# Attention with rotary embedding, then two feed-forward layers: k of two heads turned in one go, its second copy made by DMA

## The chip, the cores and the metric

The kernel runs on one core of a Trainium2 chip. The metric is the device time of one execution in microseconds; the time given is the median over several runs.

## The reference

The inputs q, k and v are float32 of shape (batch 4, heads 8, sequence 576, head dimension 64). Two feed-forward layers follow, with 2304 tokens, width 512 and inner width 2048.

```python
q_rot, k_rot = (rotate(q), rotate(k))        # rotary embedding over the 64 columns
scores = scale * np.matmul(q_rot, k_rot.transpose(0, 1, 3, 2))
scores = scores - np.max(scores, axis=-1, keepdims=True)
attn = np.exp(scores)
attn = attn / (np.sum(attn, axis=-1, keepdims=True) + 1e-09)
x = np.matmul(attn, v)                        # tokens (b, s) in rows, (h, d) in columns
h = x @ w_in;   x = (h - tanh(h)) @ w_out
h = x @ w_in2;  x = (h * sigmoid(h)) @ w_out2
```

## The kernel before

The attention works on 16 pairs of heads, one after the other, and each pair on nine steps. A step makes the scores of 128 queries of one head against all 576 keys. Steps 0 to 7 take the two heads in turn over the first 512 queries, and step 8 takes the last 64 queries of both heads. In step g TensorE makes the scores of g, turns the probabilities of step g - 2 (function `transposes`, LAG = 2), and then multiplies turned probabilities of the pair before with v (`pv`). VectorE takes the row maximum, ScalarE the exp (`exps`). The scores lie in two PSUM buffers, so the scores of step g need the exp of step g - 2 to be done. All other PSUM results of this part (turned probabilities, turned q and k, turned and spread reciprocals) share one ring of three buffers with the tag "tp".

The order of the work is written out by hand: each engine does its instructions in the order of the program text, and the one queue of SyncE (SP) that issues nearly all DMAs does so too. A wait of one instruction holds up all that stands behind it on that engine or queue.

While a pair is in work, the next pair's q and k are prepared. GpSimd rotates them (`rope_ops`, five units: q of each head, k of each head, and the remaining 64 rows of the sequence of q and k of both heads); a list of these operations is worked off over the steps, and `rope_upto` forces it up to a unit. Then TensorE turns them at the end of the steps that `QK_AT` names, so that the head dimension lies in the partitions: step 1 does q of both heads, step 3 k of the first head, step 5 k of the second, step 6 the remaining rows.

The scores are made in a split form. Each number is kept as a high part of the float32r type and the remainder. For q the high part of one head stands in 64 partitions and its remainder in the other 64 of the tile `qs`. So k must stand in both halves of the partitions, and there are two tiles of it, `kh` with the high part and `kl` with the remainder; one product with each gives q times k. To have k in both halves, `rope_dup` copies the rotated k beside itself on GpSimd before it is turned, and one turn of 128 columns yields it twice. `qk_high` turns a unit on TensorE and evicts its high parts on ScalarE at once; `qk_low` makes the remainders on VectorE one step later, after that step's row maximum. Only then is the ring buffer free.

During the attention, VectorE, ScalarE and GpSimd also convert weights of the feed-forward part from 64-bit floats, mostly in steps 7, 8 and 0. The weights come in loads of 512 KB that SP issues.

Of the kernel before, what the change touches and what calls it, by code (L numbers as in the profile page):

```python
# [8 lines left out]
F32 = mybir.dt.float32  # L9
# [4 lines left out]
ACTF = mybir.ActivationFunctionType  # L14
# [15 lines left out]
def kernel(  # L30
# [13 lines left out]
    nc = tc.nc  # L44
    B, H, S, D = q.shape
# [5 lines left out]
    NJ = S // 128  # L51
    REM = S - 128 * NJ
    MAIN = 128 * NJ
# [14 lines left out]
    PE, ACT, DVE, POOL = nc.tensor, nc.scalar, nc.vector, nc.gpsimd  # L68
# [141 lines left out]
    TPB = 3  # L210
    NPV = 4 * (NJ + 1)
    Q0 = 256
    QK_AT = {1: 0, 3: 1, 5: 2, 6: 3}
    ON_DVE = ((1, 1),)
    R_AT = (2, 4, 7)
    PV_N = (4, 0, 4, 2, 0, 4, 0, 4, 2)
# [1 line left out]
    def attention(conv, on_rope_done, on_scores_near, on_scores_done):  # L218
# [51 lines left out]
        def rope_ops(i, n, eng):  # L270
            st = {}

            def begin():
                rot = rot_t.setdefault(i, {})
                xm, xr = raw_t[i]
                if n < 2:
                    if n == 0:
                        rot[0] = rp.tile([128, NJ, 2, D], F32, tag="aq", name="aq", bufs=1)
                    st["o"] = rot[0][:, :, n, :]
                elif n < 4:  # L280
                    rot[n - 1] = rp.tile([128, NJ, 2, D], F32, tag="ak", name="ak", bufs=2)
                    st["o"] = rot[n - 1][:, :, 0, :]
                else:
                    rot[3] = rp.tile([128, 2, 2, D], F32, tag="ar", name="ar", bufs=1)
                    st["o"] = rot[3][:, :, 0, :]
                if n < 4:
                    st["b"] = rp.tile([128, NJ, D], F32, tag="bm", name="bm", bufs=3)
                    st["x"] = xm[n // 2][:, n % 2].rearrange("p (j d) -> p j d", j=NJ)
                    t = csk if n // 2 else csq
                    st["c"], st["s"] = t[:, 0], t[:, 1]  # L290
                else:
                    st["b"] = rp.tile([128, 2, D], F32, tag="br", name="br", bufs=1)
                    st["x"] = xr
                    st["c"], st["s"] = (csr[:, e].unsqueeze(1).to_broadcast([128, 2, D]) for e in range(2))
                eng.tensor_tensor(out=st["o"], in0=st["x"], in1=st["c"], op=ALU.mult)

            def cross():
                def halves(t):
                    return t.rearrange("p j (e d) -> p j e d", e=2)

                eng.tensor_tensor(out=halves(st["b"]), in0=halves(st["x"])[:, :, ::-1, :], in1=halves(st["s"]),
                                  op=ALU.mult)

            def add():
                eng.tensor_tensor(out=st["o"], in0=st["o"], in1=st["b"], op=ALU.add)

            return [begin, cross, add]

        def rope_dup(i, u):
            if u > 0:  # L310
                a = rot_t[i][u]
                if i:
                    POOL.tensor_copy(out=a[:, :, 1, :], in_=a[:, :, 0, :])
                else:
                    ACT.activation(out=a[:, :, 1, :], in_=a[:, :, 0, :], func=ACTF.Copy)

        def qk_alloc(i):
            qk_t[i] = [qkp[i % 2].tile([128, 2 * S + (REM if nm != "qs" else 0)], F32R, tag=nm, name=nm, bufs=1)
# [4 lines left out]
        KM = (slice(0, MAIN), slice(2 * S - MAIN, 2 * S))  # L323
        KO = (0, 2 * S - MAIN)
        up, dn = slice(0, 64), slice(64, 128)

        def qk_high(i, u):
            src = rot_t[i][u]
            qs, kh, kl, qr = qk_t[i]
            tp = ps.tile([128, 512], F32, tag="tp", name="tpq", bufs=TPB)  # L330
            for j in range(NJ if u < 3 else 2):
                PE.transpose(tp[:, j * 128:(j + 1) * 128], src[:, j].rearrange("p e d -> p (e d)"), ident)  # L332
            if u == 0:
                parts = [(qs[up, 0:MAIN], tp[up], qs[dn, 0:MAIN]), (qs[dn, S:S + MAIN], tp[dn], qs[up, S:S + MAIN])]
            elif u < 3:
                parts = [(kh[:, KM[u - 1]], tp, kl[:, KM[u - 1]])]
            else:
                t4 = tp[:, 0:256].rearrange("p (h s) -> p h s", h=2)
                parts = [(qr[up, h, h * 64:h * 64 + 64], t4[up, h, 0:64], qr[dn, h, h * 64:h * 64 + 64])
                         for h in range(2)]  # L340
                kc = slice(MAIN, MAIN + 128)
                parts.append((kh[:, kc].rearrange("p (h s) -> p h s", h=2), t4[:, :, 64:128],
                              kl[:, kc].rearrange("p (h s) -> p h s", h=2)))
                parts.append((kh[:, 2 * S:], t4[:, 1, 64:128], kl[:, 2 * S:]))
            for hi, t, lo in parts:
                ACT.activation(out=hi, in_=t, func=ACTF.Copy)  # L346
            return parts
# [32 lines left out]
        def exps(g):  # L380
            i, n = divmod(g, NTI)
            if n == 0:
                sum_t[i] = ap.tile([128, NTI], F32, tag="sums", name="sums", bufs=2)
            sc, st = s_t.pop(g), st_t.pop(g)
            h = tiles[n][0]
            if h != 1:
                p_t[g] = ap.tile([128, 2, S], F32, tag="p", name="p", bufs=2)
            else:
                p_t[g] = p_t[g - 1]
            p = p_t[g][:, h % 2]  # L390
            ACT.activation(out=p.rearrange("p (e s) -> p e s", e=2), in_=sc[:, :, 0:HALF],  # L391
                           func=ACTF.Exp, bias=st, accum_out=sum_t[i][:, n:n + 1])
# [127 lines left out]
        def rope_upto(i, n):  # L520
            while rq and rq[0][:2] <= (i, n):
                rq.pop(0)[2]()
# [23 lines left out]
                f()  # L546
        qk_alloc(0)
        rope_dup(0, 1)
        first = qk_high(0, 1)
        rope_dup(0, 3)  # L550
        first += qk_high(0, 0)
        first += qk_high(0, 3)
        for n in (0, 1, 5):
            qk_low([first[n]])
        parts = []
# [6 lines left out]
        while True:  # L562
            i, n = divmod(g, NTI)
            more = i + 1 < NP
            if 0 < i < NP and n == 2:
                load_v(i)
            if i + 2 < NP and n == 5:
                rope_upto(i + 1, 4)
                load_qk(i + 2)
                rope_push(i + 2)  # L570
            d = g - LAG - NTI
            i2, n2 = divmod(d, NTI)

            live = g < G

            if live:
                scores(g)
                if more and n == 0:
                    qk_alloc(i + 1)
                if g == 0:  # L580
                    parts.extend(first[2:5] + first[6:] + qk_high(0, 2))
            if 0 <= g - LAG < G:
                rest(g - LAG, g)
            if live:
                row_max(g)
            qk_low(parts)
            parts.clear()
            if 0 <= g - LAG < G:
                transposes(g - LAG)

            if more and QK_AT.get(n) == 0:
                rope_upto(i + 1, 1)
            elif more and n + 1 in QK_AT:
                rope_upto(i + 1, QK_AT[n + 1] + 1)
                rope_dup(i + 1, QK_AT[n + 1])
            if live:
                for _ in range(2 if n % 3 else 1):
                    if rq:
                        rq.pop(0)[2]()

            if 0 < i <= NP:
                at = R_AT if i < NP else (1, 2, 2)
                if n == 0:
                    recips(i - 1)
                if n == at[0]:
                    recip_rows(i - 1)
                for e in (1, 0):
                    if n == at[2 - e]:
                        recip_spread(i - 1, e)
            if d >= 0:  # L610
                if n2 == 0:
                    pvq.extend((i2, m) for m in range(NPV))
                for _ in range(PV_N[n2] if live else NPV // 2):
                    if pvq:
                        pv(*pvq.pop(0))
            rate = (CONV_RATE[n] if i else RATE_0) / 2 if live else 0.0
            conv.run(rate)
            if more and n in QK_AT:
                parts.extend(qk_high(i + 1, QK_AT[n]))
            if live:  # L620
                exps(g)
            conv.run(rate)
            if g == G - NTI:
                es_rope.close()
                es_even.close()
                on_rope_done()
            if g == G - SPLIT_AT:
                on_scores_near()
            if g == G - 1:
                es_odd.close()  # L630
                es_sc.close()
                on_scores_done()
            if g >= G:
                on_tail(g - G)
            if d > 0 and i2 == NP - 1 and not pvq:
                break
            g += 1
# [262 lines left out]
```

## Time and profile before

| what | value |
|---|---|
| time, median of 3 runs | 1146.62 us (1146.53 to 1146.91) |
| the profiled execution: its time, its span | 1147.64 us, 1145.9 us |
| share of the span that an engine is busy | TensorE 98%, weight load 79%, VectorE 69%, ScalarE 58%, GpSimd 23% |
| granted TensorE clock | 0.999 over the span |
| DMA | 98.94 MB, most of it on SP's queue, whose packets take 26.3% of 16 engines' span |
| attention, first to last scores | 13.1 to about 328 us of the span |

The span is the time from the first to the last instruction of the one profiled execution. The share of busy time is an average over the attention and the feed-forward part, which have different limits; a change in the attention is read from rows of the attention.

### The profile page before, as it was taken

How to read it: one execution, taken by the hardware profiler on the slowest of the kernel's cores; microseconds unless marked ns; L12 is line 12 of the kernel's file. 1: busy time of each engine (PE TensorE's matmuls, PEld its weight loads, DVE VectorE, ACT ScalarE, POOL GpSimd, SP SyncE). 2: the span in 40 equal slices, each digit the busy share in tenths (PEclk: the TensorE clock that was granted, in tenths of full speed). 3: DMA queues.
4: the chain of work that ended last, by engine and by line, in shares of the span. 5: the costliest groups of instructions: out<-in, count | busy, mean ns of one | idle time of the engine just before them, and what ended most of it. 6: DMA issues, size and time to landing. Idle time of an engine off the chain costs nothing.

```text
span 1145.9 us, 16928 instructions
## 1 busy us (share of the span) xinstructions
PE 1119.5 (98%) x6032; PEld 902.6 (79%) x6032; DVE 785.3 (69%) x1385; ACT 659.2 (58%) x1431; POOL 268.4 (23%) x359
## 2 busy tenths in 40 slices
PE   5999999999999999999999999999999999999998
PEld 4777777777778889888888898888888888888887
DVE  7778788787858978888899979876544533323323
ACT  4888888788866757766666657534343323222221
POOL 6566676666300101111001001111000000000000
PEclk9999999999999999999999999999999999999999
DMA  4133323232311223221333332432232203122012
GB/s 130 47 99 84 113 68 110 89 94 86 100 64 42 92 74 111 96 89 56 111 129 110 111 120 84 147 111 92 75 110 74 74 1 111 37 74 93 31 44 74
DMA packets 69588, 98.94 MB, mean 86 GB/s; under 512 B 13952, under 2 KB 50432, under 8 KB 67712
## 3 DMA queue, kind: packets, MB, share of 16 engines
q1 hardware_dynamic: 69344, 97.61, 26.3%
q8 instruction: 47, 0.77, 0.3%
q14 instruction: 37, 0.30, 0.1%
q10 hardware_dynamic: 160, 0.26, 0.1%
HBM read 74.25 MB, written 23.59 MB: 85 GB/s over the span
## 4 chain that ended last, share of the span: by engine, by line
PE 91%; DVE 4%; ACT 3%; issue 1%; DMA 0%; SPq 0%; POOL 0%; DVEq 0%; ACTq 0%
PE acc L761 35%; PE hp L685 35%; PE x L498 7%; PE tpp L466 4%; PE sc L364 3%; PE sc L365 2%; PE tpq L332 2%; PE sc L371 1%; ACT p L391 1%; DVE st L377 1%; ACT kh L346 1%; PE sc L446 1%; PE tpb L418 0%; DMA xm<-in_q_dram 0%; DVE wa L136 0%
## 5 line engine op out<-in xcount | busy, mean ns | idle before, releaser
L685 PE MATMUL hp<-xh,win 128*128 128x512 f32 (+1 forms) x1280 | 391.7, 371 | 0.0
L696 ACT ACTIVATE t<-hp 128x512 f32<-128x512 f32 (+1 forms) x160 | 89.0, 557 | 409.7 <-PE hp L685 400.0
L730 DVE TENSOR_TENSOR gl<-t,gh 128x512 fp32r<-128x512 f32 (+1 forms) x160 | 105.9, 662 | 259.5 <-ACT gh L728 259.2
L685 PEld LDWEIGHTS hp<-xh,win 128*128 128x128 f32 x1280 | 233.7, 188 | 46.8 <-issue 1.3
L685 PE MATMUL hp<-xl,win 128*128 128x512 f32 (+1 forms) x640 | 237.0, 370 | 0.0
L761 PE MATMUL acc<-gh,wout 128*128 128x512 f32 (+1 forms) x640 | 196.7, 372 | 1.2 <-ACT u L700 1.2
L761 PE MATMUL acc<-wout,gh 128*128 128x512 f32 x576 | 181.0, 395 | 0.0
L377 DVE TENSOR_REDUCE st<-sc 128x1 f32<-128x576 f32 x144 | 108.7, 755 | 60.0 <-PE sc L446 34.9
L685 PEld LDWEIGHTS hp<-xl,win 128*128 128x128 f32 x640 | 120.2, 188 | 23.2
L761 PEld LDWEIGHTS acc<-gh,wout 128*128 128x128 f32 x640 | 116.7, 188 | 24.9 <-ACT u L700 1.6
L761 PEld LDWEIGHTS acc<-wout,gh 128*128 128x128 f32 x576 | 107.1, 188 | 24.4
L761 PE MATMUL acc<-gl,wout 128*128 128x512 f32 (+1 forms) x320 | 118.9, 372 | 0.0
L153 POOL TENSOR_TENSOR win<-wa,win 128x512 fp32r<-128x512 f32 x32 | 45.4, 1419 | 292.5 <-ACT win L149 292.5
L761 PE MATMUL acc<-wout,gl 128*128 128x512 f32 x288 | 113.8, 395 | 0.0
L391 ACT ACTIVATE p<-sc,st 128x576 f32<-128x576 f32 x144 | 107.0, 743 | 9.4 <-DVE pr L434 7.2
L153 POOL TENSOR_TENSOR wout<-wa,wout 128x512 fp32r<-128x512 f32 x32 | 43.8, 1367 | 284.2 <-ACT wout L149 272.5
L432 ACT ACTIVATE pt<-tpp 128x512 f32<-128x512 f32 x144 | 86.1, 598 | 28.2 <-PE tpp L466 27.4
L728 ACT ACTIVATE gh<-t 128x512 fp32r<-128x512 f32 (+1 forms) x160 | 93.7, 586 | 1.5 <-PE acc L761 1.5
L364 PE MATMUL sc<-kh,qs 128*128 128x288 f32 x256 | 85.4, 348 | 7.1 <-ACT p L391 5.1
L466 PE MATMUL tpp<-ident,p 128*128 128x128 f32 x576 | 87.1, 274 | 0.0
L498 PE MATMUL x<-pt,vm 128*64 128x256 f32 (+1 forms) x512 | 75.8, 418 | 2.1 <-DVE xs L507 1.9
L364 PEld LDWEIGHTS sc<-kh,qs 128*128 128x128 f32 x256 | 49.2, 192 | 34.2 <-ACT p L391 17.8
(112 smaller groups left out, 1798.5 us busy)
## 6 DMA issues: line engine op xcount, KB each, us to landing
raw<-in_moe_w_in_dram SPq DMA_DIRECT2D x32, 512.0 KB, 3.6
raw<-in_moe_w_out_dram SPq DMA_DIRECT2D x32, 512.0 KB, 3.6
xin<-xd SPq DMA_DIRECT2D x14, 1024.0 KB, 4.8
pd<-xo SPq DMA_DIRECT2D x34, 256.0 KB, 2.7
xo<-pd SPq DMA_DIRECT2D x34, 256.0 KB, 4.9
xm<-in_k_dram SPq DMA_DIRECT2D x16, 256.0 KB, 2.9
xm<-in_q_dram SPq DMA_DIRECT2D x16, 256.0 KB, 3.0
vm<-in_v_dram SPq DMA_DIRECT2D x16, 256.0 KB, 2.9
```

The source lines that it names most:

```text
L153: POOL.tensor_tensor(out=w[:, 1], in0=self.val.pop(j), in1=w[:, 0].bitcast(F32), op=ALU.subtract)
L364: PE.matmul(sc[:, e, 0:HALF], lhsT=l, rhs=kh[:, c], start=True, stop=False)
L377: DVE.tensor_reduce(out=st, in_=s_t[g][:, :, 0:HALF], op=ALU.max, axis=AX.XY, negate=True)
L391: ACT.activation(out=p.rearrange("p (e s) -> p e s", e=2), in_=sc[:, :, 0:HALF], func=ACTF.Exp, bias=st, accum_out=sum_t[i][:, n:n + 1])
L432: ACT.activation(out=dst, in_=src, func=ACTF.Copy)
L466: PE.transpose(tp[:, cc * 128:(cc + 1) * 128], p[:, p0 + cc * 128:p0 + (cc + 1) * 128], ident)
L498: PE.matmul(x[o, 0:w], lhsT=l, rhs=r, start=(cc == 0), stop=(cc == NJ))
L685: PE.matmul(hp, lhsT=w[:, a, ws], rhs=bb, start=(n == 0), stop=(n == 3 * KD - 1))
L696: ACT.activation(out=t, in_=hp, func=ACTF.Tanh, scale=0.5 if l else 1.0)
L728: ACT.activation(out=gh, in_=t, func=ACTF.Copy)
L730: DVE.tensor_tensor(out=gl, in0=t, in1=gh.bitcast(F32), op=ALU.subtract)
L761: PE.matmul(acc, lhsT=a, rhs=bb, start=(fi == 0 and n == 0), stop=(fi == NH - 1 and n == 2))
```

## The change

The rotated k of both heads of the next pair is laid side by side in one tile and turned once, so that the first head comes out in the upper 64 partitions and the second in the lower 64. The remaining rows of q and k are treated likewise: one turn instead of two. High parts and remainders are then made of each head in its own 64 partitions alone, and eight DMAs from SBUF to SBUF, issued on SP's queue in step 6, bring each head's `kh` and `kl` to the other 64 partitions, and the remaining rows of the second head to a second place. GpSimd's copies are gone. The turns stand in steps 1, 3 and 5, and step 6 has none; k of both heads must be rotated by step 3. In each step ScalarE does the exp first and the evictions of turned q and k after it. The first pair is prepared as before.

```diff
-    QK_AT = {1: 0, 3: 1, 5: 2, 6: 3}
+    QK_AT = {1: 0, 3: 1, 5: 2}
...
+                elif n < 4 and i:
+                    if n == 2:
+                        rot[1] = rp.tile([128, NJ, 2, D], F32, tag="ak", name="ak", bufs=2)
+                    st["o"] = rot[1][:, :, n - 2, :]
...
-                    st["o"] = rot[3][:, :, 0, :]
+                    st["o"] = rot[3][:, 0] if i else rot[3][:, :, 0, :]
...
-                if i:
-                    POOL.tensor_copy(out=a[:, :, 1, :], in_=a[:, :, 0, :])
-                else:
-                    ACT.activation(out=a[:, :, 1, :], in_=a[:, :, 0, :], func=ACTF.Copy)
+                ACT.activation(out=a[:, :, 1, :], in_=a[:, :, 0, :], func=ACTF.Copy)
...
+        def qk_turn(i, u):
+
+            src = rot_t[i][(0, 1, 3)[u]]
+            qs, kh, kl, qr = qk_t[i]
+            tp = ps.tile([128, 512], F32, tag="tp", name="tpq", bufs=TPB)
+            for j in range(NJ if u < 2 else 1):
+                PE.transpose(tp[:, j * 128:(j + 1) * 128], src[:, j].rearrange("p e d -> p (e d)"), ident)
+            if u == 0:
+                return [(qs[up, 0:MAIN], tp[up], qs[dn, 0:MAIN]), (qs[dn, S:S + MAIN], tp[dn], qs[up, S:S + MAIN])]
+            if u == 1:
+                return [(kh[up, KM[0]], tp[up], kl[up, KM[0]]), (kh[dn, KM[1]], tp[dn], kl[dn, KM[1]])]
+            k0, k1 = slice(MAIN, S), slice(S, S + REM)
+            return [(qr[up, 0, 0:64], tp[up, 0:64], qr[dn, 0, 0:64]),
+                    (qr[dn, 1, 64:128], tp[dn, 0:64], qr[up, 1, 64:128]),
+                    (kh[up, k0], tp[up, 64:128], kl[up, k0]), (kh[dn, k1], tp[dn, 64:128], kl[dn, k1])]
+
+        def k_copies(i):
+            for t in qk_t[i][1:3]:
+                nc.sync.dma_start(out=t[dn, 0:S].bitcast(F32), in_=t[up, 0:S].bitcast(F32))
+                nc.sync.dma_start(out=t[up, S:2 * S].bitcast(F32), in_=t[dn, S:2 * S].bitcast(F32))
+                for o in (up, dn):
+                    nc.sync.dma_start(out=t[o, 2 * S:].bitcast(F32), in_=t[dn, S:S + REM].bitcast(F32))
...
+            return parts
+
+        def qk_evac(parts):
             for hi, t, lo in parts:
                 ACT.activation(out=hi, in_=t, func=ACTF.Copy)
             return parts
...
             qk_low(parts)
             parts.clear()
+            if more and n - 1 == max(QK_AT):
+                k_copies(i + 1)
...
-                rope_upto(i + 1, QK_AT[n + 1] + 1)
-                rope_dup(i + 1, QK_AT[n + 1])
+                rope_upto(i + 1, QK_AT[n + 1] + 2)
...
             if more and n in QK_AT:
-                parts.extend(qk_high(i + 1, QK_AT[n]))
+                parts.extend(qk_turn(i + 1, QK_AT[n]))
             if live:
                 exps(g)
+            qk_evac(parts)
```

## Rows read from the trace of the kernel before

**Rows 1.** Busy time of each engine, pairs 1 to 14; then clock, DMA share, GB/s

```profile
33.59:307.89 274.30, 268.43 (x1991) 205.42 (x1991) 217.35 (x440) 227.99 (x577) 175.36 (x268) 1.00 0.29 86
```

**Rows 2.** Timeline of TensorE, twelfth pair (start us, us, what)

```profile
242.51 0.66 PE L332 MATMUL tpq<-ident,ak 128*128 128x128 f32 x4
242.92 0.38 PE L364 MATMUL sc<-kh,qs 128*128 128x288 f32 x1
...
244.57 0.40 PE L364 MATMUL sc<-kh,qs 128*128 128x288 f32 x1 [0.23 <-ACT p L391]
...
245.67 0.42 PE L418 MATMUL tpb<-rt,sel 128*128 128x128 f32 x2
...
248.56 0.38 PE L364 MATMUL sc<-kh,qs 128*128 128x288 f32 x1
248.78 0.29 PE L365 MATMUL sc<-kl,qs 128*128 128x288 f32 x1
```

**Rows 3.** Timeline of TensorE, last pair: first products of steps 6 and 7

```profile
320.68 0.40 PE L364 MATMUL sc<-kh,qs 128*128 128x288 f32 x1
...
321.67 0.38 PE L364 MATMUL sc<-kh,qs 128*128 128x288 f32 x1
```

**Rows 4.** Timeline of ScalarE, twelfth pair

```profile
241.93 0.60 ACT L432 ACTIVATE pt<-tpp 128x512 f32<-128x512 f32 x1 [0.93 <-PE tpp L466]
243.20 0.60 ACT L346 ACTIVATE kh<-tpq 128x512 fp32r<-128x512 f32 x1 [0.68 <-PE tpq L332]
243.69 0.74 ACT L391 ACTIVATE p<-sc,st 128x576 f32<-128x576 f32 x1
...
244.89 0.32 ACT L346 ACTIVATE qr<-tpq 64x64 fp32r<-64x64 f32 x2
...
245.36 0.74 ACT L391 ACTIVATE p<-sc,st 128x576 f32<-128x576 f32 x1
```

**Rows 5.** Timeline of VectorE, twelfth pair

```profile
241.49 0.76 DVE L377 TENSOR_REDUCE st<-sc 128x1 f32<-128x576 f32 x1 [1.39 <-PE sc L446]
...
243.72 0.76 DVE L377 TENSOR_REDUCE st<-sc 128x1 f32<-128x576 f32 x1 [0.53 <-PE sc L365]
244.40 0.68 DVE L351 TENSOR_TENSOR kl<-tpq,kh 128x512 fp32r<-128x512 f32 x1
...
246.29 0.35 DVE L351 TENSOR_TENSOR qr<-tpq,qr 64x64 fp32r<-64x64 f32 x2
```

**Rows 6.** Timelines of GpSimd and TensorE, step 3 of the fifth pair

```profile
97.39 0.74 POOL L305 TENSOR_TENSOR ak<-ak,bm 128x256 f32<-128x256 f32 x1
...
98.47 0.60 PE L332 MATMUL tpq<-ident,ak 128*128 128x128 f32 x4
```

**Rows 7.** Timeline of SP's queue, ninth and twelfth pairs (issue, not transfer)

```profile
175.96 1.12 SPq L267 DMA_DIRECT2D vr<-in_v_dram  x2
...
179.08 0.63 SPq L251 DMA_DIRECT2D xr<-in_q_dram  x1
...
243.62 0.42 SPq L512 DMA_DIRECT2D xd<-xs  x1
244.14 7.76 SPq L115 DMA_DIRECT2D raw<-in_moe_w_out_dram  x2
```

**Rows 8.** DMA issues: count, KB each, median us from issue to landing

```profile
xm<-in_q_dram SPq DMA_DIRECT2D x16, 256.0 KB, 3.0
...
xd<-xs SPq DMA_DIRECT2D x32, 128.0 KB, 2.0
...
xd<-xs SPq DMA_DIRECT2D x16, 32.0 KB, 1.7
```

**Rows 9.** Timeline of all engines, step 4 of the ninth pair

```profile
178.66 0.60 PE L466 MATMUL tpp<-ident,p 128*128 128x128 f32 x4
...
178.87 0.75 ACT L391 ACTIVATE p<-sc,st 128x576 f32<-128x576 f32 x1
```

**Rows 10.** Timeline of VectorE, thirteenth pair: a weight's first conversion

```profile
266.89 0.42 DVE L129 TENSOR_SCALAR wa<-raw 128x512 int32<-128x512 int32 x1
```

More of the change, by code (lines that the diff above doesn't have):

```diff
@@ L548, in attention @@
         rope_dup(0, 1)
-        first = qk_high(0, 1)
+        first = qk_evac(qk_high(0, 1))
         rope_dup(0, 3)
-        first += qk_high(0, 0)
-        first += qk_high(0, 3)
+        first += qk_evac(qk_high(0, 0))
+        first += qk_evac(qk_high(0, 3))
         for n in (0, 1, 5):
@@ L580, in attention @@
                 if g == 0:
-                    parts.extend(first[2:5] + first[6:] + qk_high(0, 2))
+                    parts.extend(first[2:5] + first[6:] + qk_evac(qk_high(0, 2)))
             if 0 <= g - LAG < G:
```

## The prediction

> **What bounds the kernel now.** I read the busy times of a stretch first, then the timelines of single engines over one pair of heads, then the queue that issues DMAs. Over pairs 1 to 14 of the attention TensorE is busy 268.4 of 274.3 us, ScalarE 228.0, VectorE 217.4, GpSimd 175.4 [rows 1]. [...] So a step of this stretch lasts as long as TensorE's list for it, unless something holds that list up.
>
> [...]
>
> In the twelfth pair, the quiet one that I work with, the four turned tiles of the next pair stand at the end of steps 1, 3, 5 and 6. Step 5 ends with four transposes for the second head's k, from 242.51 to 242.92. Step 6 ends with two for the rests; the scores of step 7 begin only at 244.57, after 0.23 us of waiting for an exp [rows 2]. In the last pair nothing is turned, and there step 6 takes 321.67 − 320.68 = 0.99 us [rows 3], against 244.57 − 242.92 = 1.65 [rows 2]. TensorE's own list and that wait make the step, then, and taking work from it shortens it.
>
> **The change part by part**, per pair; 15 pairs are turned this way.
>
> *Transposes.* 14 become 9. Step 5 has one instead of four. The four cost 242.92 − 242.51 = 0.41 us, so one some 0.11; saved 0.30 (bounds: 0, if one costs as much as the group, and 0.41). Step 6 has none: 1.65 − 0.99 = 0.66 saved, as the last pair shows. Together 0.96, times 15 = 14.4 us. Steps 1 and 3 keep their four.
>
> *Exp before the evictions.* The 0.66 holds only if the scores of step 7 find their buffer free, which the exp of step 5 frees. Before, ScalarE waited 0.68 us for the transposes, evicted k at 243.20 and began that exp at 243.69 [rows 4]. Now it can begin when the eviction of 241.93 has passed (0.49 us a piece, by 243.20 to 243.69) and the row maximum of 241.49 is there (242.25) [rows 4, 5]: at 242.42, done by 243.16. Step 7 now wants to begin at 242.92 − 0.30 + 0.99 = 243.61. So the wait goes. In steps 1 and 3 the exp also comes earlier, but nothing waited for it, and I give it nothing.
>
> *Evictions and remainders.* Eight evictions and eight remainders a pair, as before, only elsewhere. Step 3 evicts two halves of 64 rows where it had one tile, some 0.5 us more on ScalarE and 0.7 on VectorE in step 4; both idle just after, 0.93 us before 241.93 and 1.39 before 241.49 [rows 4, 5], and that hides it. Uncovered it would cost up to 0.7 a pair. The four small remainders of the rests move from step 7 to step 6. VectorE reaches them after step 6's row maximum, which began 243.72 − 242.92 = 0.80 after the scores: now at 242.62 + 0.80 + 0.68 = 244.10. Four at 0.35 for two last till 244.80 [rows 5]. They free the last of three tp buffers, and by the order of allocation the next in need of it is the spread of reciprocals of step 7, which TensorE reaches 245.67 − 244.57 = 1.10 after step 7's start, at 244.71. So a new wait of some 0.10 (bounds 0 and 0.4): −1.5 us in all.
>
> *GpSimd* loses three copies. The second head's rotated k must now be there by step 3, not step 5. In the tightest pair it ends at 97.39 + 0.74 = 98.13 and step 3's transposes begin at 98.47 [rows 6]; a copy that stood ahead of it goes, so the margin grows. Cost nothing; if the cover failed, a few tenths of a us in some pairs.
>
> *Eight DMAs a pair.* This is the part without a row of its own: SBUF to SBUF, 64 rows. For kh and then for kl: 64 x 576 words (144 KB) down, 144 KB up, and two small ones. They go into SP's queue in step 6, behind the stores of the attention's output. The last of those issued at 243.62, and the next DMA followed at 244.14 [rows 7]. By then the evictions that kh needs are done (four take 245.36 − 244.89 = 0.47 after the exp, so 243.63) [rows 4], and kl's remainders (244.80) come in time for the fifth. Issue costs per DMA: the nearest rows are 64-row loads, 1.12 for two, or 0.56, and 0.63; the 128-row store took 0.42 [rows 7]. I take 0.56, since rows of 64 partitions are nearest. kl's first copy, the fifth, goes out at 244.14 + 4 x 0.56 = 246.38.
>
> Landing: a 128 KB store takes 2.0 us, a 32 KB one 1.7, a 256 KB load 3.0 [rows 8]. I take 2.0, the nearest size: 248.38. Bounds 1.7 and 3.0.
>
> Who needs it: dependencies here go by region (a transposition of one half of a p tile ran at 178.66, before the exp that writes the other half, issued earlier, at 178.87 [rows 9]), so the next pair's first scores wait for kl's first copy alone. They begin at 243.61 + (248.56 − 244.57 = 3.99) + 0.10 = 247.70, and their first product with kl 0.22 later (248.78 − 248.56) [rows 2], at 247.92. TensorE then stands 248.38 − 247.92 = 0.46 us at each pair's start: −6.9 us. Behind it on TensorE stands everything, so this is lost in full.
>
> What waits behind the eight in SP's queue: the weight load that went at 244.14 goes some 4.5 us later. What it brings is first converted at 266.89 [rows 10], so nothing is lost. The feed-forward part after the attention is unchanged and runs on TensorE without a gap, so what the attention saves arrives at the end.
>
> *Sum.* Per pair 0.30 + 0.66 − 0.10 − 0.46 = 0.40, times 15 = 6.0 us. The profiled execution took 1147.64 (span 1145.9 and 1.7 around it), 1.0 above the median of 1146.62; 1141.6 for such an execution, and **1140.6** for the median.
>
> **The rivals.**
>
> *The copies land in time.* If they issue in the store's 0.42 [rows 7] and land in 2.0, kl's first is there at 244.14 + 1.68 + 2.0 = 247.82, before 247.92. Then 0.86 x 15 = 12.9: **1133.7**. For it: these copies never leave the core's memory. Against it: each 64-row row seen took over 0.5 to issue.
>
> *64 rows move at half the rate.* From 32 to 128 KB a store takes 0.3 us more [rows 8], so 1.6 fixed and 0.3 for each 96 KB at 128 rows. At half that rate 144 KB takes 0.9, and the copy lands after 2.5, at 248.88. The wait is 0.96, the pair loses 0.10, in all +1.5: **1148.1**, no change that can be measured. For it: no large 64-row transfer is in the trace that would exclude it. Against it: the same rows say that most of the 2 us is fixed.
>
> [...]
>
> *The copies are late for good (the other side).* Place: the same wait at the next pair's start. At 0.63 an issue and the 3.0 of the 256 KB load the copy lands at 244.14 + 2.52 + 3.0 = 249.66, the wait is 1.74, the pair loses 0.88: +13.2, **1159.8**. It decides from a landing past 248.78 on, where 0.86 is used up; past 248.93 the loss can be measured (2.3 us over 15 pairs). For it: three large copies, two of them just ahead, share the DMA engines with it. Against it: those engines are busy 29% in this stretch [rows 1].
>
> **How the numbers follow.** Wait of about half a us, 1140.6: 0.45. In time, 1133.7: 0.22. Half rate, 1148.1: 0.17. Late, up to 1159.8: 0.16. A measurement of this kernel tells about 0.2%, 2.3 us, from no change. The first two are faster (0.67), the third is the same (0.17), the fourth slower (0.16). The range runs from 1132, the second case with no wait for remainders (14.4 saved), to 1149, just past the third; the fourth is left out. The likeliest case's own range is 1136 to 1144.
>
> **What would show it.** Step 6 at 0.99 and step 5 some 0.30 shorter show the transposes right. The exp of step 5 ahead of the small evictions, and no wait for it before step 7, show the reordering right. At the start of each pair, TensorE idle before the first product with kl, released by a DMA, shows the copies' price: 0.46 expected, nothing in the second case, about 1 in the third, more in the fourth. A wait for VectorE before the spread of step 7 of 0.1 shows the buffer's. I am wrong if step 1 to 5 grow, if GpSimd's rope is late for step 3, or if the wait at the pair's start moves elsewhere, such as to later steps' kh.

## The result and the profile after

The changed kernel takes 1164.32 us (median of 4 runs, 1161.76 to 1165.68) against 1146.76 (1146.53 to 1147.12): a ratio of 1.0150, 95% interval 1.0134 to 1.0166. It is slower by 17.6 us where 6.0 us of gain were predicted. The profiled execution has a span of 1163.0 us, 17.1 more than before. From the first scores of the last step to the end of the span both traces need the same 821.7 us, so the whole difference arises in the attention.

The windows view over pairs 1 to 14 of the kernel after:

```profile
33.95:324.68 290.73, 270.11 (x1923) 200.94 (x1922) 230.88 (x440) 238.24 (x578) 163.29 (x225) 0.99 0.42 115
```

Against [rows 1] the stretch is 16.4 us longer with TensorE busy for about as long: 270.1 of 290.7 us, where it was 268.4 of 274.3. TensorE now stands still for 20.6 us instead of 5.9. The DMA engines are busy 42% instead of 29%. The mean granted clock is 0.99, not 1.00; outside two stretches, which are shown below, it is 1.00.

Where it stands still, the waits view of the kernel after says (engine and line that waits, on what; total us, times, longest), PEld and PE being the weight load and the product of one and the same matmul:

```profile
PEld sc L392 <- DMA kl<-kl: 21.2, 15, 2.7
PE sc L392 <- DMA kl<-kl: 18.0, 15, 2.5
```

The kernel before has no such wait. It comes 15 times, once for each pair that is turned in the new way, and TensorE loses 18.0 us in it.

Twice more was lost than the length of the wait. The first products with kl in the second and third pair, with the wait before them, and then the windows view of the stretches in which the clock was granted at 0.50, soon after each of these two products:

```profile
36.82 0.40 PE L392 MATMUL sc<-kl,qs 128*128 128x288 f32 x1 [2.49 <-DMA kl<-kl]
...
57.26 0.40 PE L392 MATMUL sc<-kl,qs 128*128 128x288 f32 x1 [1.89 <-DMA kl<-kl]
```

```profile
38.02:41.43 3.41, 3.41 (x18) 3.36 (x17) 2.34 (x8) 2.65 (x7) 0.00 (x0) 0.50 0.76 228
58.50:61.91 3.41, 3.41 (x15) 2.23 (x16) 1.79 (x6) 2.51 (x5) 0.00 (x0) 0.50 0.50 154
```

TensorE is busy all through both, only at half the clock: four transposes of a p tile took 0.60 us before the first of them and 1.06 in it.

```profile
37.42 0.60 PE L493 MATMUL tpp<-ident,p 128*128 128x128 f32 x4
...
39.11 1.06 PE L493 MATMUL tpp<-ident,p 128*128 128x128 f32 x4
```

In these two pairs steps 1 and 2 of the second and steps 0 and 1 of the third are longer by some 3.2 us beyond the wait. The kernel before has no such fall in its attention. Of the four executions of the kernel after, the one with a granted clock of 1.000 has the shortest span, 1160.0 us; the three at 0.995 to 0.997 have 1162.1 to 1163.9.

TensorE's timeline of the kernel after, the twelfth pair ([rows 2] for before), the start of the thirteenth, and the last pair [rows 3]:

```profile
241.49 0.38 PE L391 MATMUL sc<-kh,qs 128*128 128x288 f32 x1
243.66 0.40 PE L392 MATMUL sc<-kl,qs 128*128 128x288 f32 x1 [1.80 <-DMA kl<-kl]
...
256.92 0.33 PE L334 MATMUL tpq<-ident,ar 128*128 128x128 f32 x1
257.01 0.38 PE L391 MATMUL sc<-kh,qs 128*128 128x288 f32 x1
...
257.98 0.38 PE L391 MATMUL sc<-kh,qs 128*128 128x288 f32 x1
...
259.29 0.44 PE L445 MATMUL tpb<-rt,sel 128*128 128x128 f32 x2
...
260.67 0.40 PE L398 MATMUL sc<-kh,qr 128*128 128x288 f32 x1
...
262.20 0.38 PE L391 MATMUL sc<-kh,qs 128*128 128x288 f32 x1
263.69 0.40 PE L392 MATMUL sc<-kl,qs 128*128 128x288 f32 x1 [1.11 <-DMA kl<-kl]
...
337.80 0.40 PE L391 MATMUL sc<-kh,qs 128*128 128x288 f32 x1
...
338.79 0.38 PE L391 MATMUL sc<-kh,qs 128*128 128x288 f32 x1
```

The reader is to see three things. Step 6 lasts 257.98 − 257.01 = 0.97 us, where it took 1.65 [rows 2] and the last pair, where nothing is turned, takes 0.99 before and after: that saving came. At 262.20 the thirteenth pair's first product with kh begins, and 0.22 later the first with kl should; it begins 1.49 later, so 1.27 are lost to the copy of kl. Step 7 lasts 260.67 − 257.98 = 2.69 instead of 2.46 in most pairs before.

The first scores of a step mark its start on TensorE's timeline; a step lasts to the next start. The differences to the kernel before, summed over the pairs, in us, from one profiled execution of each kernel:

| step | after | kl second | early, zeros | old order | order alone | by unit | by unit, q later | by unit alone | by unit, conversion in 5 | by unit, conversion in 3 |
|---|---|---|---|---|---|---|---|---|---|---|
| 0 | +21.7 | +0.8 | +0.5 | +12.0 | 0.0 | +1.6 | +1.6 | +0.2 | +6.3 | +1.2 |
| 1 | +2.5 | +0.6 | +0.5 | +0.5 | 0.0 | +0.7 | +0.3 | +0.1 | +1.8 | +0.7 |
| 2 | −0.6 | +3.3 | +4.8 | +0.8 | −0.7 | +3.3 | +5.0 | +0.4 | −0.7 | −0.9 |
| 3 | +1.5 | +2.6 | +4.1 | −0.2 | +2.4 | 0.0 | 0.0 | −0.2 | −0.1 | −1.2 |
| 4 | −0.3 | +0.4 | −0.1 | +0.8 | +0.1 | +0.8 | +0.7 | 0.0 | +0.8 | +1.6 |
| 5 | −3.7 | −3.7 | −3.7 | −4.9 | +0.1 | −4.9 | −4.9 | 0.0 | −4.9 | −4.4 |
| 6 | −8.3 | −6.8 | −6.6 | +7.1 | −7.0 | −9.7 | −9.7 | −6.9 | −8.9 | −8.8 |
| 7 | +4.3 | +5.3 | +5.1 | −0.4 | +0.4 | +2.6 | +0.2 | +0.4 | +4.6 | +3.6 |
| 8 | 0.0 | 0.0 | 0.0 | −0.7 | +1.0 | 0.0 | +2.5 | +1.0 | +10.8 | +0.5 |

The columns behind the first are the experiments below. Two of the profiled executions were the longest of their kernel's runs, so that their columns are dearer than the median: the old order (1162.68 against 1158.51) and the conversion in 5 (1157.37 against 1154.48). In the first column, steps 5 and 6 gain 12.0 us of the 14.4 predicted, and step 0 alone loses 21.7, or 1.44 a pair, where 0.46 were predicted; 0.95 of the 21.7 is the slower clock of the third pair.

SP's queue of the kernel after at the end of the twelfth pair, the row of before being in [rows 7] (start us, time of issue, what):

```profile
258.01 0.61 SPq L539 DMA_DIRECT2D xd<-xs  x1
258.71 0.51 SPq L346 DMA_DIRECT2D kh<-kh  x1
259.31 0.55 SPq L347 DMA_DIRECT2D kh<-kh  x1
259.91 1.23 SPq L349 DMA_DIRECT2D kh<-kh  x2
261.23 0.54 SPq L346 DMA_DIRECT2D kl<-kl  x1
...
263.73 0.58 SPq L115 DMA_DIRECT2D raw<-in_moe_w_out_dram  x1
```

and the page's list of DMA issues and chain of waits, after (count, KB each, median us from issue to landing; [rows 8] has the stores and loads of before):

```profile
PE 87%; DVE 5%; DMA 3%; ACT 3%; issue 1%; SPq 1%; POOL 0%; DVEq 0%; ACTq 0%
...
kh<-kh SPq DMA_DIRECT2D x30, 144.0 KB, 2.4
kl<-kl SPq DMA_DIRECT2D x30, 144.0 KB, 2.4
```

kl's first copy, the fifth of the eight, goes out at 261.23, which is 2.52 after the first. So one copy costs the queue 0.63 us, not the 0.56 assumed. It goes out 4.22 after step 6's start (3.76 were predicted) and lands 2.4 later, not 2.0. DMA now has 3% of the chain that sets the end.

ScalarE and VectorE of the kernel after, around step 7 of the twelfth pair [rows 4, 5]:

```profile
256.97 0.75 ACT L418 ACTIVATE p<-sc,st 128x576 f32<-128x576 f32 x1
...
257.71 0.43 ACT L373 ACTIVATE qr<-tpq 64x64 fp32r<-64x64 f32 x2
258.15 0.46 ACT L373 ACTIVATE kh<-tpq 64x64 fp32r<-64x64 f32 x2
258.64 0.60 ACT L459 ACTIVATE pt<-tpp 128x512 f32<-128x512 f32 x1
```

```profile
257.82 0.76 DVE L404 TENSOR_REDUCE st<-sc 128x1 f32<-128x576 f32 x1 [0.23 <-PE sc L392]
258.65 0.46 DVE L378 TENSOR_TENSOR qr<-tpq,qr 64x64 fp32r<-64x64 f32 x2
259.12 0.48 DVE L378 TENSOR_TENSOR kl<-tpq,kh 64x64 fp32r<-64x64 f32 x2
```

The spread of step 7 starts on TensorE at 259.29. ScalarE's eviction of step 6's turned probabilities ends at 259.24, and VectorE's remainders only at 259.60. So the spread waits for ScalarE, which reached that eviction late because the four small ones stood ahead of it. The prediction had put this wait down to the remainders.

### The profile page after: what moved, and what is told of

Read it like the earlier page. It is cut to its first block, busy times and chain, and to the rows that moved or that the text cites. A ratio compares the mean times of both kernels' runs of the same rounds, so it can differ in the third digit from the quotient of the medians.

```text
span 1163.0 us, 16984 instructions
## 1 busy us (share of the span) xinstructions
PE 1120.4 (96%) x5957; PEld 897.3 (77%) x5957; DVE 798.0 (69%) x1385; ACT 669.7 (58%) x1431; POOL 255.8 (22%) x314
## 4 chain that ended last, share of the span: by engine, by line
PE 87%; DVE 5%; DMA 3%; ACT 3%; issue 1%; SPq 1%; POOL 0%; DVEq 0%; ACTq 0%
PE acc L790 35%; PE hp L714 34%; PE x L525 6%; PE tpp L493 3%; DMA kl<-kl 3%; PE sc L391 3%; PE sc L392 2%; DVE st L404 1%; PE tpq L334 1%; ACT p L418 1%; ACT kh L373 1%; DVE pr L461 0%; DVE kl L378 0%; PE sc L473 0%; ACT pt L459 0%
## 5 line engine op out<-in xcount | busy, mean ns | idle before, releaser
L392 PE MATMUL sc<-kl,qs 128*128 128x288 f32 x256 | 75.6, 309 | 18.5 <-DMA kl<-kl 18.0
```

What stands on the lines that cost most here:

```text
L392: PE.matmul(sc[:, e, 0:HALF], lhsT=l, rhs=kl[:, c], start=False, stop=True)
```

## The experiments

Three theories were put to the test. "Late": the fifth place in the queue and a landing above 2 us make kl's copy late, and all of the loss is that wait. "Crowded": the extra traffic of large copies slows other transfers or engines. "Exp first costs": the order on ScalarE, the exp ahead of the evictions, loses elsewhere.

**kl's first copy in second place.** The same eight DMAs, in the order in which the next pair needs them.

```diff
             for t in qk_t[i][1:3]:
                 nc.sync.dma_start(out=t[dn, 0:S].bitcast(F32), in_=t[up, 0:S].bitcast(F32))
+            for t in qk_t[i][1:3]:
                 nc.sync.dma_start(out=t[up, S:2 * S].bitcast(F32), in_=t[dn, S:2 * S].bitcast(F32))
+            for t in qk_t[i][1:3]:
                 for o in (up, dn):
```

> The eight copies in another order: the first large one of kh, then the first large one of kl, then the other two large ones, then the four small ones. Theory 'late' (the first copy of kl goes out fifth, 4 x 0.62 us after the first, lands 2.4 us later, and the first scores of the next pair wait for it): it goes out about 2.4 us after the start of step 6, as soon as its remainders are made, instead of 4.05, lands at 4.8, before the scores at 5.2; step 0 goes back to about 2.3 us, the 21.7 us lost there come back nearly all, 1140 to 1146 us. Theory 'crowded' (eight DMAs more on the queue and on the DMA engines slow down whatever stands near them): the order changes little, 1157 to 1164 us.

1150.31 us (1150.07 to 1151.79), ratio 1.0031 (1.0019 to 1.0042). One copy moved from the fifth place to the second gives back 14 us: step 0 falls from +21.7 to +0.8. "Late" explains that step, but it had expected a time at or under 1146, and this kernel is still 3 us slower than the one before. Two waits of it that were smaller before or not there:

```profile
PE x L527 <- DVE xs L536: 5.8, 7, 1.3
...
PEld tpb L447 <- ACT pt L461: 4.5, 14, 0.3
```

The first is the products of step 2, which wait for an x that VectorE evicts; before, 1.9. The second is step 7's wait for ScalarE, 0.3 a pair. Neither has to do with a copy's landing.

**The same DMAs early, from a tile of zeros.** The eight issue in step 1, so that no landing can be late.

```diff
-                nc.sync.dma_start(out=t[dn, 0:S].bitcast(F32), in_=t[up, 0:S].bitcast(F32))
-                nc.sync.dma_start(out=t[up, S:2 * S].bitcast(F32), in_=t[dn, S:2 * S].bitcast(F32))
+                nc.sync.dma_start(out=t[dn, 0:S].bitcast(F32), in_=zz[up, 0:S])
+                nc.sync.dma_start(out=t[up, S:2 * S].bitcast(F32), in_=zz[dn, 0:S])
...
-            if more and n - 1 == max(QK_AT):
+            if more and n == 1:
```

> The same eight DMAs in count, size and partitions, but issued in step 1 and from a tile of zeros, so that nothing waits for them late; the other 64 rows of k are zeros and the products lack that part. Theory 'late': no wait at the start of a pair, 1136 to 1141 us, somewhat below the reordered copies. Theory 'crowded': the DMAs are all still there, so the time stays above 1150 us.

1152.01 us (1150.29 to 1153.06), ratio 1.0042 (1.0027 to 1.0057). Step 0 is at +0.5, and the losses in steps 2, 3 and 7 are there as in the run above. So they do not come from copies that land late. The time alone decides nothing between the theories: "Late" had expected 1136 to 1141, and "Crowded" over 1150. The run with the traffic alone, below, decides it.

**The old order on ScalarE.** The kernel after, with the evictions ahead of the exp again.

```diff
-                parts.extend(qk_turn(i + 1, QK_AT[n]))
+                parts.extend(qk_evac(qk_turn(i + 1, QK_AT[n])))
             if live:
                 exps(g)
-            qk_evac(parts)
```

> The changed kernel with the evictions of turned q and k ahead of the exp again. Theory 'late': the wait for kl stays; steps 6 and 7 lose some of what they won, 1164 to 1168 us. Theory 'exp first costs' (the later evictions make remainders late and hold the ring of three buffers, the 0.36 us in step 3, 0.2 in step 6 and 0.35 in step 7 of five pairs): faster than the changed kernel by 3 to 6 us, 1158 to 1161 us.

1158.51 us (1157.60 to 1162.68), ratio 1.0098 (1.0081 to 1.0114): faster than the kernel after. TensorE's timeline of this kernel, first scores of step 7:

```profile
256.48 0.40 PE L391 MATMUL sc<-kh,qs 128*128 128x288 f32 x1 [0.91 <-ACT p L418]
```

The wait for the exp is back, at 0.91, and step 6 loses 7.1 us. But steps 3 and 7 lose nothing any more. Step 0 loses 12.0 instead of 21.7: TensorE waits for kl 9 times (8.9 us) instead of 15 (18.0). That a longer step 6 leaves the copies more time fits this, but was not tested by itself. The granted clock was 1.00 in the whole attention, so the price of the slower clock is gone too. The order on ScalarE thus gains in step 6 and costs in step 3, and together with the single turn in step 7.

**The order alone.** The kernel before, with the exp ahead of the evictions everywhere.

```diff
+            return parts
+
+        def qk_evac(parts):
             for hi, t, lo in parts:
...
                 exps(g)
+            qk_evac(parts)
```

> The kernel before with only the exp put ahead of the evictions; two turns of k, no copies by DMA. My prediction's own step: the wait before the scores of step 7 (0.4 us a pair) goes, minus a wait for the ring, 1140 to 1144 us. Theory 'exp first costs': the same waits in steps 3, 6 and 7 as in the changed kernel, 1146 to 1150 us.

1144.18 us (1143.69 to 1144.92), ratio 0.9974 (0.9965 to 0.9983). Step 6 gains 7.0 us without any turn saved. In the twelfth pair it takes 241.02 − 239.84 = 1.18 us, where it took 1.65 [rows 2], and two transposes still end it:

```profile
239.84 0.38 PE L367 MATMUL sc<-kh,qs 128*128 128x288 f32 x1
...
240.88 0.38 PE L332 MATMUL tpq<-ident,ar 128*128 128x128 f32 x2
241.02 0.38 PE L367 MATMUL sc<-kh,qs 128*128 128x288 f32 x1
```

So of the 0.66 a pair that the prediction gave to step 6, 7.0 / 15 = 0.47 belong to the order and 0.19 to the two transposes. Step 3 loses 2.4.

**The traffic alone.** The kernel before, with six unused copies a pair issued in step 6: four of 64 rows by 576 words and two of 128 rows by 288 words, 144 KB each.

```diff
...
+            if more and n == 6:
+                up, dn = slice(0, 64), slice(64, 128)
+                for z in zc:
+                    nc.sync.dma_start(out=z[dn], in_=za[up])
+                    nc.sync.dma_start(out=z[up], in_=za[dn])
+                for z in zd:
+                    nc.sync.dma_start(out=z, in_=za[:, 0:HALF])
```

> The kernel before, and in step 6 of each pair six DMAs more on SP's queue, between tiles that nothing else uses: four of 64 rows x 576 words, as the change has them, and two of 128 rows x 288 words, the same 144 KB each. Theory 'late' (copies cost only where something waits for them): 1146 to 1149 us. Theory 'crowded': 1150 us and more. Beside it: if 64 rows move at half the rate of 128, the packets of 2304 bytes take about twice the time per byte of those of 1152, and the landing differs by about 0.4 us.

1147.03 us (1146.40 to 1148.73), ratio 1.0001 (0.9992 to 1.0011). "Crowded" falls: copies that nobody waits for cost nothing here. The page's DMA issues of this kernel:

```profile
zc<-za SPq DMA_DIRECT2D x60, 144.0 KB, 2.5
...
zd<-za SPq DMA_DIRECT2D x30, 144.0 KB, 2.3
```

For the same bytes 64 rows land after 2.5 us and 128 rows after 2.3. Issue takes mostly 0.59 to 0.60 for both shapes. So a copy from SBUF to SBUF of 128 rows is as slow to issue as one of 64, and the 64 rows, by which the prediction had argued, are not the reason.

**The order by unit.** The second order of the copies, and the exp ahead of the evictions in steps 5 and 6 only; in steps 1 and 3 the evictions go first, as before.

```diff
...
+            late = []
             if more and n in QK_AT:
-                parts.extend(qk_turn(i + 1, QK_AT[n]))
+                turned = qk_turn(i + 1, QK_AT[n])
+                parts.extend(turned)
+                if QK_AT[n] < 2:
+                    qk_evac(turned)
+                else:
+                    late = turned
...
-            qk_evac(parts)
+            qk_evac(late)
```

> The reordered copies, and on ScalarE the evictions of q (step 1) and of k (step 3) ahead of the exp again, only those of the rests (step 5) behind it. Theory 'exp first costs, in steps 1 and 3': the waits in steps 3, 4 and before step 7's scores go (2.6, 0.4 and 2.5 us in all), the one before the spread of step 7 stays: 1143 to 1146 us. Theory 'what is left is VectorE, late with the weights' (waits for the evicted x in step 2): 1148 us and more.

1141.45 us (1139.73 to 1142.12), ratio 0.9948 (0.9931 to 0.9965): faster than before by some 5.5 us, about the gain that the prediction had named. Step 3's loss is gone, steps 5 and 6 gain 14.6. Left over are steps 2 (+3.3) and 7 (+2.6).

**q's small evictions later still.** In addition, of the four small evictions the two of k come first, and the two of q, with their remainders, stand behind step 6's turned probabilities.

```diff
+            return [(kh[up, k0], tp[up, 64:128], kl[up, k0]), (kh[dn, k1], tp[dn, 64:128], kl[dn, k1]),
+                    (qr[up, 0, 0:64], tp[up, 0:64], qr[dn, 0, 0:64]),
+                    (qr[dn, 1, 64:128], tp[dn, 0:64], qr[up, 1, 64:128])]
...
-            qk_low(parts)
+            qk_low([x for x in parts if x not in held])
...
+            qk_low(qk_evac(held))
+            held.clear()
...
-            qk_evac(late)
+            qk_evac(late[:2])
+            held.extend(late[2:])
```

> As the last, and of the four small evictions of the rests the two of k come first, the two of q only behind step 6's turned probabilities. Theory 'small evictions hold up the spread' (TensorE waits in step 7 for ScalarE's eviction of step 6, which stands behind four small ones): that wait of 0.35 us a pair goes too, 1137 to 1141 us, faster than the kernel before. Theory 'VectorE late': gains there come back as waits in step 2, 1144 us and more.

1143.59 us (1142.20 to 1143.88), ratio 0.9967 (0.9955 to 0.9978). Step 7's wait went (+0.2), as it should if ScalarE's small evictions hold it up; the gain came back as +2.5 in step 8 and +5.0 in step 2. In all it is 2.1 us slower than the kernel by unit, where a gain had been expected.

**The order by unit alone.** The kernel before, four turns as they were, no copies, and the exp ahead in steps 5 and 6 only.

```diff
...
+            late = []
             if more and n in QK_AT:
-                parts.extend(qk_high(i + 1, QK_AT[n]))
+                turned = qk_high(i + 1, QK_AT[n])
+                parts.extend(turned)
+                if QK_AT[n] < 2:
+                    qk_evac(turned)
+                else:
+                    late = turned
             if live:
                 exps(g)
+            qk_evac(late)
```

> The kernel before, two turns of k and no copies by DMA, with the exp ahead of the evictions in steps 5 and 6 only. If the order is worth the wait before step 7's scores (0.46 us in 14 pairs) and costs only in steps 1 and 3: 1139 to 1142 us. If the order's worth in steps 5 and 6 is bound to its cost elsewhere: 1144 us, like the exp ahead everywhere.

1141.99 us (1141.12 to 1142.91), ratio 0.9957 (0.9942 to 0.9972). This is the run to remember: the order on ScalarE alone gives what the order and the single turn give together. What the turn saves on TensorE, some 0.33 in step 5 and 0.19 in step 6, or 7.8 us over 15 pairs, is used up, mostly in steps 0, 2 and 7: these three are 6.5 us longer in the kernel by unit than here.

**One conversion moved to step 5**, in three kernels: in the one by unit, in the order by unit alone, and in the kernel before. The list says how many steps of the conversion each of the nine steps of a pair does.

```diff
-    CONV_RATE = (1.6, 0.0, 0.0, 0.0, 0.0, 0.0, 0.0, 1.5, 1.5)
+    CONV_RATE = (0.6, 0.0, 0.0, 0.0, 0.0, 1.0, 0.0, 1.5, 1.5)
```

> The reordered copies with the evictions of q and k ahead of the exp (as two runs ago), and one of the weight conversion's micro steps moved from step 0 to step 5 of each pair (4.6 a pair as before). Theory 'VectorE late with the weights': the waits for the evicted x in step 2 (5.8 us in all, 2.3 in the kernel before) shrink, 1136 to 1139 us, faster than the same without the move (1141.5). Rival 'the micro step only moves the wait' (a wait in steps 5 to 7 instead): 1141 us and more.

> The kernel before with the exp ahead in steps 5 and 6 only, and the same micro step moved. Theory 'turning k once pays when VectorE has room': this gains at most the 2.3 us that the kernel before waits in step 2, 1139.5 to 1142 us, and stays behind the version with k turned once. Rival 'turning once pays nothing': equal to it.

> The kernel before with the micro step moved alone. If the moved step is worth its waits in step 2 alone: 1144 to 1147 us.

1154.48 (ratio 1.0058, 1.0045 to 1.0072), 1143.46 (0.9967, 0.9956 to 0.9979) and 1146.99 us (0.9995, 0.9986 to 1.0004). The first is slower by 13 us than the kernel by unit, where a gain had been expected. SP's queue of this kernel in one of the four pairs that lost most:

```profile
150.24 0.38 SPq L111 DMA_DIRECT2D raw<-in_moe_w_in_dram  x1
150.73 0.51 SPq L346 DMA_DIRECT2D kh<-kh  x1
```

and what TensorE then did:

```profile
156.76 0.37 PE L393 MATMUL sc<-kh,qs 128*128 128x288 f32 x1 [2.71 <-DMA kh<-kh]
```

The moved conversion frees its buffer earlier, so a 512 KB weight load now goes out 0.49 us ahead of the copies. The first copy lands after 4.9 to 5.9 us instead of 2.3 in those four pairs, and TensorE stands still for 2.71 in this one. After three of the four waits the granted clock fell to 0.50 again, as here, soon after the product above:

```profile
158.05:161.46 3.41, 3.41 (x16) 1.95 (x15) 2.68 (x5) 1.32 (x3) 3.33 (x5) 0.50 0.41 135
```

That is part of the +6.3 in step 0. Without copies the move costs little or nothing, and the gain expected of the second run did not come: 1143.46 against 1141.99 for the order by unit alone, with overlapping intervals. The kernel before did not change.

**One conversion moved to step 3 instead**, well ahead of the copies, in the kernel by unit.

```diff
-    CONV_RATE = (1.6, 0.0, 0.0, 0.0, 0.0, 0.0, 0.0, 1.5, 1.5)
+    CONV_RATE = (0.6, 0.0, 0.0, 1.0, 0.0, 0.0, 0.0, 1.5, 1.5)
```

> This is the kernel with k turned once, the copies in the order high part, low part, high part, low part, and exp ahead of the evictions of turned q and k in steps 5 and 6 only; in addition one conversion step of the background weight conversion is moved from step 0 to step 3, where VectorE has no work of the pair's evictions of x. Theory 'VectorE late': the 3.3 us that the matmuls of x lose in step 2 to the evicted x come from VectorE's conversions in step 0 that run longer; with one of them moved away step 2 goes back to within 1.5 us of before over the 15 pairs, and the time is 1136 to 1140 us. Rival 'the wait only moves': the moved conversion delays step 3 or the copies' wait comes back in step 0, step 2 gains but another step loses as much, and the time is 1141 us or more.

1139.90 us (1139.56 to 1140.81), ratio 0.9936 (0.9923 to 0.9950): the fastest of all. Step 2 goes from +3.3 to −0.9. The wait that did it, first in the kernel by unit and then in this one:

```profile
PEld x L527 <- DVE xs L536: 7.3, 8, 1.7
```

```profile
PEld x L527 <- DVE xs L536: 1.6, 2, 0.8
```

So the loss in step 2 came from VectorE's conversions in step 0, behind which the eviction of x stood. Against the order by unit alone (1141.99) the single turn is now ahead by 2.1 us; the two intervals overlap, and the order alone was not run with its conversion in step 3, so a gain of the single turn is not shown.

## Why the prediction was wrong

**The step that failed is the price of the eight DMAs**, and with it the choice of the likeliest case. The place, the mechanism and what stands behind it were right: TensorE stands at each pair's start before the first product with kl, released by a DMA. The size was 1.27 in the twelfth pair and 1.44 on average (1.38 without the slower clock), not 0.46. Three terms make it up for the twelfth pair. The first copy goes out 1.70 after step 6's start, not 1.52; the store ahead of it takes 0.61 to issue, and kh's evictions end 1.60 after that start, not 1.01. Four issues take 4 × 0.63 and not 4 × 0.56. The landing takes 2.42 and not 2.0. Together 0.18 + 0.28 + 0.42 = 0.88, less some 0.1 by which the next pair begins later.

Both dear values were in the text, but in different rivals: 0.63 an issue in the fourth, a landing of 2.5 in the third. Taken together they give 244.14 + 4 × 0.63 + 2.5 = 249.16, so a wait of 249.16 − 247.92 = 1.24, close to the 1.27 measured in that pair. I had treated as alternatives two uncertainties that add. The fourth rival was therefore the right one by its mechanism and by its place, with 1.74 for the wait where 1.44 was measured. That its 1159.8 comes nearest to the time measured is luck in part: its wait is too long by some 4.4 us in all, and it lacks 8.3 us of losses in other steps, which the table below has.

That alone would have given 1152 by the prediction's own sum (0.96 − 0.10 − 1.24 = −0.38 a pair, 5.7 us slower). From 5.7 to the 17.1 of the spans:

| term | predicted | measured | us in all |
|---|---|---|---|
| step 0, other pairs dearer than the twelfth | 1.24 a pair, as just worked out | 1.44 | +3.0 |
| step 7, the spread's wait | 1.5 | 4.3 | +2.8 |
| steps 5 and 6, TensorE's saving | 14.4 | 12.0 | +2.4 |
| steps 1 to 4 | 0 | 3.1 | +3.1 |

These make 11.3, and with 5.7 the sum is 17.0. Some 3.2 of the 11.3 are the slower clock after the two waits shown above, which the prediction did not have at all: 0.95 of it in the row of step 0, the rest in that of steps 1 to 4.

**Transposes.** Right. Step 5 is shorter by 0.33 in the quiet pair (predicted 0.30), step 6 by 0.68 (predicted 0.66). The sums fall short of 14.4 mainly by the first pair, where step 5 grows by 0.89 and step 6 by 0.23 instead of both shrinking, which makes 2.1 us. In five other pairs step 6 takes 1.18 and not 0.97, which makes 1.0; the rest of the pairs gain a little more than predicted. In the kernel by unit the first pair's step 5 is 0.32 shorter than before, so its growth belongs to the order in steps 1 and 3.

**Exp before the evictions.** Right for step 6, and worth more than it was credited with: 0.47 of the 0.66. "In steps 1 and 3 the exp also comes earlier, but nothing waited for it, and I give it nothing" left out a cost: with the order alone step 3 is 2.4 us longer, and with the order by unit alone it is not.

**Remainders.** The new wait before the spread was foreseen, at 0.10, and it measured 0.2 to 0.4. In the twelfth pair its cause was not VectorE's remainders, since the spread began at 259.29, before they ended at 259.60, but ScalarE's eviction of the turned probabilities, which ended at 259.24 behind four small evictions. With two of those four moved behind it the wait goes; that edit moves two remainders as well, so it does not separate the two by itself.

**GpSimd.** Right: in the fifth pair of the kernel after, the second head's k is there 2.2 us ahead of the transposes, as its timeline and TensorE's show [rows 6]:

```profile
105.18 0.72 POOL L309 TENSOR_TENSOR ak<-ak,bm 128x256 f32<-128x256 f32 x1
```

```profile
108.11 0.60 PE L334 MATMUL tpq<-ident,ak 128*128 128x128 f32 x4
```

**What waits behind the copies.** Right: the weight load went out at 263.73, 5.0 after the first copy where some 4.5 were predicted, and the waits view has no conversion that waits for a load [rows 10]. Regions were right too [rows 9]: the next pair's first product with kl began at 263.69, and the last two of kl's copies went out from 262.46 to 263.69, to land 2.0 after their issue (median).

**The rival of half the rate.** Half the rate was assumed, and no run shows it. In the run with unused copies a packet of a 64-row copy (2304 bytes) took 180 ns in the median (168 in the kernel after) and one of a 128-row copy (1152 bytes) 54 ns, 1.67 times as long per byte, but the two packets differ in size as well as in rows. In the landing it makes 0.2 us, 2.5 against 2.3, and so a small part of the error. The rival's own landing of 2.5 was near the 2.4 of the kernel after.

**The bound.** That TensorE's list makes the steps was right (98% busy in [rows 1]), with one thing left out: in this kernel the slack of the other engines is a few tenths of a us at certain places, and a shorter list on TensorE uses it up. Step 7 lost at once (+4.3 over the pairs), and step 2 as soon as step 0 no longer did (+3.3).

What stays open: why kl's first copy takes 3.2 to 3.4 us to land in three of the pairs, why the clock fell after a wait of 1.89 us at the start of the third pair and not after one of 1.91 at that of the fifth, and why step 4 loses 0.7 to 1.6 in the kernels by unit.

## What to carry to other kernels

Work that is taken from the bounding engine and given to a queue of DMAs is paid for by the place in that queue (here the second place instead of the fifth gave back 14 us): count every issue ahead of the one that is needed first, add its landing, take the dear value of both at once, and issue in the order of need. Behind a wait of the engine that bounds the kernel, look at the granted clock: here it fell to 0.50 behind two of the 15, which cost some 3.2 us beyond the waits. When one edit holds two changes, run each alone: here a reordering of a few lines on ScalarE carried most of the gain, and the larger part of the edit carried the loss. Where an engine does two kinds of work, choose which goes first step by step, by who waits for it.

## What the runs showed of the hardware

A copy from SBUF to SBUF took SP's queue some 0.6 us, 0.59 to 0.60 with 64 as with 128 rows in the run with unused copies and 0.63 in the kernel after, where in the kernel before a store of 128 rows, 32 KB, took 0.42 [rows 7]. In the kernel after it landed after 2.4 us for 144 KB and 1.9 to 2.0 for 16 KB (medians). Behind a load of 512 KB issued 0.49 us earlier on the same queue, in the kernel by unit with the conversion in step 5, the first copy landed after 4.9 to 5.9.

The granted clock of TensorE fell from 1.00 to 0.50 five times in the attention, twice in the kernel after and three times in the one by unit with the conversion in step 5. Each time TensorE had just begun again behind a wait of 1.9 to 2.7 us for a copy. It was busy all through each of these stretches, and four transposes took 1.06 us instead of 0.60.

In some of the places where VectorE and GpSimd ran at the same time their operations took longer. In the kernel by unit, on VectorE and on GpSimd:

```profile
147.70 1.76 DVE L136 SCALAR_TENSOR_TENSOR wa<-raw,wa 128x512 int32<-128x512 int32 x1
...
227.79 0.63 DVE L136 SCALAR_TENSOR_TENSOR wa<-raw,wa 128x512 int32<-128x512 int32 x1
```

```profile
147.64 1.27 POOL L153 TENSOR_TENSOR win<-wa,win 128x512 fp32r<-128x512 f32 x1 [1.83 <-ACT win L149]
...
227.78 1.78 POOL L153 TENSOR_TENSOR wout<-wa,wout 128x512 fp32r<-128x512 f32 x1 [2.31 <-ACT wout L149]
```

The same two operations meet twice. The first time VectorE starts 0.06 us after GpSimd and takes 1.76 us, GpSimd 1.27. The second time they start within 0.01, and VectorE takes 0.63 and GpSimd 1.78. The first time it is VectorE that is longer, by 1.1 us, the second time GpSimd, by 0.5. In the kernel before, 32 of the 64 runs of this operation of VectorE overlap with none of GpSimd and take 0.67 to 0.70 us; the other 32 take 0.63 to 1.76. Why some of these take longer no run here shows. That in a kernel with a few tenths of slack such a meeting can make an eviction behind it late is my estimate; no run here separates it from the place of the conversion itself.
